# Seven groups' second layer by seven block products instead of three, and q and k cast to bf16 by GpSimd's loads

## The chip, the core and the metric

The kernel runs on one core of a Trainium2 chip. TensorE (PE) multiplies, VectorE (DVE), ScalarE (ACT) and GpSimd (POOL) do the rest, SyncE (SP) issues most transfers. The metric is the device time in microseconds of one launch, the median of several runs. A profile is of one further execution; it has its own time, and a span from its first to its last instruction.

## The reference

```python
def _attn_ref(q, k, v, w_phi):          # q, k, v: 8 batches x 8 heads x 576 x 64
    def phi(x):
        proj = np.einsum('bhsd,df->bhsf', x, w_phi)             # 128 features
        proj = proj - np.max(np.abs(proj), axis=-1, keepdims=True)
        return np.concatenate([np.exp(proj), np.exp(-proj)], axis=-1)
    q_p, k_p = (phi(q), phi(k))
    kv = np.einsum('bhsf,bhsd->bhfd', k_p, v)
    z = np.sum(k_p, axis=2)
    num = np.einsum('bhsf,bhfd->bhsd', q_p, kv)
    den = np.einsum('bhsf,bhf->bhs', q_p, z)[..., None] + 1e-06
    return num / den

def _moe_ref(x, g_ln, w_ch1, w_ch2):    # x: 8 x 576 x 512, the heads side by side
    mu = np.mean(x, axis=-1, keepdims=True)
    var = np.mean((x - mu) ** 2, axis=-1, keepdims=True)
    xn = (x - mu) / np.sqrt(var + 1e-06) * g_ln
    ch = np.maximum(xn @ w_ch1, 0.0) @ w_ch2                    # 512 -> 2048 -> 512
    return x + ch
```

All inputs and the output are fp32; the kernel multiplies in bf16.

## The kernel before

Attention runs over 32 units of two heads each, numbered 0 to 31. A unit's q and k are cast to bf16 and transposed (`qkT`), projected (`pm` for the maxima and for k, `pt` for q), put through exponentials (`eb` of k, `ea` of q), v is scaled by the keys' factors into `vv` on GpSimd (L1101 to L1107), then PE forms the key-value products in `n_bank` (L1162, L1168), the numerators (`num`, L1226, L1232), VectorE adds and inverts (`numc`, `rden`), and GpSimd writes x. The first 512 tokens of a head lie four to a partition; its last 64, the tail, are loaded apart (`qx`, `vx`).

The feed-forward part runs over nine groups of 512 token rows, 0 to 8, in four tiles of 128 tokens. The first layer (`hT_ps`, L1530; for group 0 L1387) gives 16 blocks of 128 hidden values into the ring `hT`. The second layer of group g is multiplied while the first layer of g + 1 runs. In groups 0 to 5 it is plain: per tile 16 matmuls of 512 columns into `ch_ps` (L1562), and one result per tile, on VectorE (L1570) or on ScalarE with the addition of x on GpSimd (L1575, L1579). In groups 6, 7 and 8 (`FAST`) it goes by seven block products instead of eight (`fast`, L1698): two token tiles, even and odd hidden blocks and two column halves make the blocks. It needs sums of blocks of w2, made once into T buffers (`weight_sums`, L1613), and sums of blocks of the hidden values into S buffers (`token_sums`, L1635), four for each pair of tiles and each half of the hidden blocks. A product is 8 matmuls of 256 columns, a group has 14; each product ends in one half-width result on VectorE (L1707). The T and S buffers are laid over the loaded q, k and v (`qk_bufs`, `v_bufs`), each pair of tiles with an S set of its own.

Loads: q, k and v of units 0 to 7 come on SP, 256 KB each, later ones 512 KB for two units (`load_main`, L577). Weights come in four transfers issued by GpSimd, which cast to bf16 on the way: two for w1 (L670), two for w2 (L688). Loads of units 8 to 15 wait for the second half of w1. Units 0 to 7 are transposed by PE. From unit 8 on (`a_trans_dma`) the loaded fp32 q and k are cast into one of three `b16` buffers, the main part by whichever of VectorE, ScalarE or GpSimd the list names (L797, L802, L804), the tail by another instruction, and a transposing transfer on SP (L823) fills one of four `qkT` buffers.

The order of every engine's instructions is fixed: the program makes a list of operations with their costs, `ORDER` names for each engine the operations in their order, and `Order.run` lays them out in time by a model of costs, lags and transfers, which decides how the engines' instructions are recorded against each other and where PE gets filler matmuls (L2172, before 75 us). `SLACK` and the costs in `dma` are numbers of that model.

## Time and profile before

| | |
|---|---|
| median of 3 runs | 355.04 us (355.03 to 356.68) |
| the profiled execution: time, span | 353.76 us, 352.0 us |
| busy: PE, DVE, ACT, POOL | 339.7, 296.1, 253.5, 192.7 us |
| granted PE clock, mean | 0.998 |
| moved | 53.87 MB; read from HBM 36.77 MB, written 9.44 MB |
| q and k loads of 512 KB on SP | 12 and 12, median 5.6 and 6.4 us to landing |
| main casts of q and k: POOL, ACT, DVE | 13 at 1.89, 10 at 1.07, 1 at 1.21 us |

A profile line of grouped instructions gives the source line, engine, operation, what is written and read, shapes and count, then busy time, the mean of one in ns, and the idle time before them with what ended it. Lines of windows give busy time and instruction count for each engine in a stretch, then the clock, the DMA share and GB/s. Matmuls are pipelined: the duration of one is longer than the distance to the next, so distances are read from the chain of waits, whose rows give start, length and what.

### The profile page before, as it was taken

To read this page: it belongs to the slowest core of one execution; us is meant where nothing else is said; L and a number is where in the kernel's file an instruction comes from. 1 tells how busy PE (TensorE), PEld (TensorE's weight loads), DVE (VectorE), ACT (ScalarE), POOL (GpSimd) and SP (SyncE) were. 2 spreads that over 40 slices of the span, in tenths; PEclk is the share of its full clock that TensorE was granted. 3 is DMA by queue.
4 is the path that set the end of the run, shared out by engine and by line. 5 is a ranking of instruction groups with operands and counts; after the bars stand their busy time and mean duration, and the time that the engine had idled before them with its cause. 6 is when DMAs were issued, how large, how long until landed. Compare 5 with 4: busy or idle time off the path is not lost.

```text
span 352.0 us, 9056 instructions
## 1 busy us (share of the span) xinstructions
PE 339.7 (97%) x3482; PEld 216.1 (61%) x3482; DVE 296.1 (84%) x670; ACT 253.5 (72%) x561; POOL 192.7 (55%) x250
## 2 busy tenths in 40 slices
PE   8887998999999999999999999999999999999995
PEld 7766785655555555464555455555555578488884
DVE  5799984999889889878896799799768699999994
ACT  4997988878999887869776958798676840554410
POOL 5487367849952584667292696987668630000000
PEclk9999999999999999999999999999999999999999
DMA  7999999994997939859809993705061123500053
GB/s 206 277 297 214 212 236 232 254 198 58 266 270 183 248 96 216 160 105 209 281 16 190 284 281 64 136 0 125 10 128 58 62 67 61 148 33 3 7 114 119
DMA packets 93675, 53.87 MB, mean 153 GB/s; under 512 B 61104, under 2 KB 88048, under 8 KB 93632
## 3 DMA queue, kind: packets, MB, share of 16 engines
q1 hardware_dynamic: 89392, 47.72, 57.2%
q0 software_dynamic: 3328, 4.49, 7.4%
q10 hardware_dynamic: 912, 1.08, 0.9%
q8 instruction: 27, 0.44, 0.5%
q14 instruction: 16, 0.13, 0.1%
HBM read 36.77 MB, written 9.44 MB: 131 GB/s over the span
## 4 chain that ended last, share of the span: by engine, by line
PE 82%; DMA 8%; DVE 3%; issue 2%; POOL 2%; ACT 2%; SPq 1%; ACTq 0%; POOLq 0%
PE hT_ps L1530 27%; PE ch_ps L1562 23%; PE ch L1698 10%; DMA w<-in_moe_w_ch_dram 6%; PE pm L1017 4%; PE n_bank L1168 4%; PE sum L1881 3%; PE num L1226 3%; PE pt L1026 2%; DMA qk<-in_q_dram 2%; POOL vv L1101 1%; PE n_bank L1162 1%; PE n_bank L1226 1%; ACT ea L914 1%; PE n_bank L1232 1%
## 5 line engine op out<-in xcount | busy, mean ns | idle before, releaser
L1530 PE MATMUL hT_ps<-xT,w 128*128 128x512 bf16 x432 | 103.9, 380 | 0.0
L1562 PE MATMUL ch_ps<-w,hT 128*128 128x512 bf16 x384 | 89.7, 380 | 1.2 <-DMA w<-in_moe_w_ch_dram 1.2
L1101 POOL TENSOR_TENSOR vv<-v,ek 128x1024 bf16<-128x1024 f32 x32 | 61.2, 1912 | 49.6 <-issue 32.9
L1074 DVE TENSOR_REDUCE m<-pm 128x8 f32<-128x1024 f32 x60 | 72.3, 1214 | 14.2 <-PE pm L1017 13.1
L1094 ACT ACTIVATE eb<-pm 128x1024 bf16<-128x1024 f32 x64 | 64.5, 1044 | 4.8 <-DVE m L1074 3.0
L1138 ACT ACTIVATE ea<-pt 128x1024 bf16<-128x1024 f32 x56 | 56.1, 1045 | 11.1 <-PE pt L1026 10.9
L1530 PEld LDWEIGHTS <-w 128*128 128x128 bf16 x432 | 38.1, 97 | 39.2 <-issue 1.9
L1562 PEld LDWEIGHTS <-hT 128*128 128x128 bf16 x384 | 35.0, 97 | 39.8 <-issue 2.5
L1540 ACT ACTIVATE hT<-hT_ps 128x512 bf16<-128x512 f32 x64 | 37.7, 608 | 18.6 <-PE hT_ps L1530 18.4
L1293 POOL TENSOR_TENSOR x<-numc,rden 128x128 bf16<-128x128 f32 (+1 forms) x56 | 33.6, 615 | 18.6 <-DVE rden L1260 18.6
L1538 DVE TENSOR_SCALAR hT<-hT_ps 128x512 bf16<-128x512 f32 x44 | 29.7, 679 | 5.4 <-PE hT_ps L1530 5.2
L1226 PEld LDWEIGHTS <-ea 128*128 128x128 bf16 x448 | 21.6, 97 | 8.5 <-issue 0.3
L804 POOL TENSOR_TENSOR b<-qk,one 128x1024 bf16<-128x1024 f32 x13 | 24.5, 1890 | 2.3 <-DMA v<-in_v_dram 2.3
L1168 PE MATMUL n_bank<-vv,eb 128*128 128x65 bf16 x512 | 23.8, 194 | 0.0
L1168 PEld LDWEIGHTS <-eb 128*128 128x128 bf16 x512 | 21.3, 98 | 2.2
L1248 DVE TENSOR_TENSOR numc<-num,em 128x390 f32<-128x390 f32 (+1 forms) x32 | 17.0, 530 | 6.6 <-PE num L1226 5.9
L1434 DVE BATCH_NORM_STATS2 st<-x 128x6 f32<-128x512 bf16 (+1 forms) x40 | 21.9, 567 | 0.4 <-POOL x L1293 0.4
L1017 PE MATMUL pm<-wbk,qkT 64*128 64x128 bf16 x448 | 19.9, 218 | 0.2 <-DVE xT L962 0.2
L1107 POOL TENSOR_TENSOR vv<-vx,ek 128x260 bf16<-128x260 f32 x32 | 19.9, 623 | 0.0
L1017 PEld LDWEIGHTS <-qkT 64*128 64x128 bf16 x448 | 13.8, 94 | 9.6 <-issue 6.5
L1579 POOL TENSOR_TENSOR o<-o,x 128x512 f32<-128x512 f32 x13 | 15.0, 1158 | 7.8 <-ACT o L1575 6.9
L1254 DVE TENSOR_TENSOR numc<-numc,num 128x390 f32<-128x390 f32 (+1 forms) x32 | 17.0, 533 | 0.7
(180 smaller groups left out, 659.7 us busy)
## 6 DMA issues: line engine op xcount, KB each, us to landing
out_dram<-o SPq DMA_DIRECT2D x29, 256.0 KB, 3.1
qk<-in_q_dram SPq DMA_DIRECT2D x12, 512.0 KB, 5.6
qk<-in_k_dram SPq DMA_DIRECT2D x12, 512.0 KB, 6.4
v<-in_v_dram SPq DMA_DIRECT2D x12, 512.0 KB, 5.2
w<-in_moe_w_ch_dram POOLq DMA_DIRECT2D x4, 1024.0 KB, 10.4
qk<-in_k_dram SPq DMA_DIRECT2D x8, 256.0 KB, 6.1
qk<-in_q_dram SPq DMA_DIRECT2D x7, 256.0 KB, 5.9
v<-in_v_dram SPq DMA_DIRECT2D x7, 256.0 KB, 6.7
```

The source lines that it names most:

```text
L1017: nc.tensor.matmul(ps[:, half * 4 + c, :], u["qkT"][rows, cols], wbk[rows, half, :], start=True, stop=True,)
L1074: nc.vector.reduce_max(out=m, in_=ps, axis=AX.X, apply_absolute_value=True)
L1094: nc.scalar.activation(eb, ps, AF.Exp, scale=(1.0, -1.0)[t])
L1101: eng.tensor_tensor(out=u["vv"][:, :, 0:MX, 0:D], in0=bcast(vb[:, hh, :].rearrange("p (c d) -> p c d", d=D), 1, 2), in1=bcast(e[:, :, 0:MX ...
L1138: nc.scalar.activation(u["EA"][:, t, 0:1024], u["pt"], AF.Exp, scale=(1.0, -1.0)[t])
L1168: nc.tensor.matmul(ps[:, t, c // 4, :], EB[:, t, c, :], vv[:, t, c, :], start=False, stop=(t == 0 and c == MX - 1), skip_group_check=True,)
L1226: nc.tensor.matmul(ps[t][:, i, :], ea(u, t, c), KV[:, t, c // 4, :], start=True, stop=True,)
L1293: eng.tensor_tensor(out=dst, in0=src, in1=by, op=ALU.mult)
L1530: nc.tensor.matmul(st["ps"], w1_sb[:, kc, jj * P : (jj + 1) * P], xT_bufs[g % XB][:, kc::KC, :], start=(kc == 0), stop=(kc == KC - 1),)
L1540: nc.scalar.activation(h_sb, st["ps"], AF.Relu)
L1562: nc.tensor.matmul(ch[g, i], hT[g, jj][:, i * P : (i + 1) * P], w2_sb[:, jj, :], start=(jj == 0), stop=(jj == JC - 1),)
L1698: nc.tensor.matmul(sums(), left(c), right(c), start=(begin and c == 0), stop=(c == CP - 1), skip_group_check=True,)
```

## The change

1. `FAST` becomes groups 2 to 8. Groups 2 to 5 (below `FULL`) use one S set for both pairs of tiles, and work the pairs one after the other: all products of tiles 0 and 1, then the sums and products of tiles 2 and 3. Their sums go to two PSUM banks per pair, half a bank for each output block.
2. From unit 8 on the main parts of q and k are loaded by GpSimd straight into `b16`, cast on the way: two loads of 256 KB (fp32) per unit. Their 24 loads of 512 KB on SP and their 24 casts go; v and all tails stay. `qk_bufs` are free after unit 7, so the T sums are made earlier.
3. Token sums may be made by GpSimd as well as by VectorE.
4. A new `ORDER` for all engines, and other numbers in the model (`SLACK`, the lags of GpSimd's loads).

```diff
-SLACK = ((0.22, 0.0, 0.0, 0.97), (0.35, 0.6, 1.6, 0.97), (0.22, -1.15, 0.0, 1.07))
+SLACK = ((0.22, 0.6, 0.8, 1.0), (0.35, 1.2, 2.2, 1.0), (0.22, -1.15, 0.0, 1.07))
...
-    FAST = (LAST - 2, LAST - 1, LAST)
+    FAST = range(2, LAST + 1)
+    FULL = LAST - 2
...
-        def cast_main(engine):
-            cast(
-                engine, b16[:, 0 : MX * P].rearrange("p (i f) -> p i f", i=2),
-                qk_bufs[u["g"] % NBUF][:, :, u["hh"], :],
+        def load_cast(i):
+            b, h, step = heads(u["pair"], u["i"], 0)
+            t = (q, k)[i]
+            nc.gpsimd.dma_start(
+                out=b16[:, i * 4 * P : (i + 1) * 4 * P].rearrange("p (a f) -> p a f", a=2),
+                in_=bass.AP(
+                    tensor=t.tensor, offset=t.offset + (b * H + h) * S * D,
+                    ap=[[4 * D, P], [S * D, 2], [1, 4 * D]],
+                ),
             )
...
-        add(("DVE", "ACT", "POOL"), (1.13, 0.937, 1.852), rank, cast_main, r=[*loaded(u, "q"), *loaded(u, "k")],
-            w=[("b16", n % NB16)])
-        dma("SP", rank, 0, turn, r=[("b16x", n % NB16), ("b16", n % NB16)],
+        for i in range(2):
+            dma("POOL", rank, 262144, lambda i=i: load_cast(i), w=[("b16" + "qk"[i], n % NB16)], us=0.7, row=1024)
...
+        dma("SP", rank, 0, turn, r=[("b16x", n % NB16), ("b16q", n % NB16), ("b16k", n % NB16)],
...
-    def token_sums(g, c):
+    def token_sums(g, c, only=None):
-        for p in range(NM // 2):
+        for p in range(NM // 2) if only is None else (only,):
+            z = p if g >= FULL else 0
...
-                nc.vector.tensor_tensor(out=out_, in0=a, in1=b, op=op)
+                eng = nc.vector if engine == "DVE" else nc.gpsimd
+                eng.tensor_tensor(out=out_, in0=a, in1=b, op=op)
...
-                add("DVE", Port(0.335), (), lambda i=i, f=sums: f(i),
+                add(("DVE", "POOL"), (Port(0.335), 1.08), (), lambda e, i=i, f=sums: f(i, e),
...
+        if lean:
+            cols, bank = chain % 2 * FH, chain // 2
...
+        if lean:
+            took = ("B", 1) if i in (0, 3) and cs[0] == 0 else None
+            gave = ("B", 1) if i in (5, 6) else None
...
+    def fast_steps(lean=False):
...
+        if lean:
+            return [
+                (p, i, cs) for p in pairs_
+                for i, cs in [(i, cs) for cs in (h1, h2) for i in range(2)]
+                + [(i, range(CP)) for i in range(2, 7)]
+            ]
...
+                    if g - 1 < FULL and 2 * step == len(steps):
+                        for c in (0, SH):
+                            token_sums(g - 1, c, 1)
...
-                for key in "kqv":
+                for key in "kqv" if m < QK_DMA else "v":
                     load_main(key, m + i, 1 if m < H else HG, rank, "SP")
```

How the lists move is shown for GpSimd at three places. The first is its beginning, from the load of the normalization's weights to the `vv` of unit 0 (before, with the start of unit 1's). Before:

```order
L658 DMA gln_85<-in_moe_g_ln_dram 128x4x1
L1101 TENSOR_TENSOR vv_335<-v0_101,ek_320 128x2x8x64
L1106 CAST vv_335<-ek_320 128x2x8
L1107 TENSOR_TENSOR vv_335<-vx0_106,ek_320 128x2x130
L1101 TENSOR_TENSOR vv_423<-v0_101,ek_401 128x2x8x64
```

And now (`b16_2`, `b16_0` and `b16_1` are the buffers of units 8, 9 and 10):

```order
L678 DMA gln_85<-in_moe_g_ln_dram 128x4x1
L838 DMA b16_2_147<-in_q_dram 128x2x256
L838 DMA b16_0_145<-in_k_dram 128x2x256
L838 DMA b16_2_147<-in_k_dram 128x2x256
L838 DMA b16_1_146<-in_q_dram 128x2x256
L1126 TENSOR_TENSOR vv_322<-v0_101,ek_309 128x2x8x64
L1131 CAST vv_322<-ek_309 128x2x8
L1132 TENSOR_TENSOR vv_322<-vx0_106,ek_309 128x2x130
```

Four loads of q and k, for units 8, 9 and 10, stand ahead of the first `vv`; the rest of the beginning keeps its order up to the first half of w1, which comes one instruction sooner. On PE the second half of w1 is first used 8 block matmuls (L1387), one unit's key-value products and five small transposes later than before; on SP one more v load of 256 KB stands behind that half.

The second place is the loads of w2, around the `vv` of units 4 and 5. Before:

```order
L688 DMA w2_133<-in_moe_w_ch2_dram 128x8x512
L986 TENSOR_TENSOR x_156<-xT2_140 128x2x2x64
L1101 TENSOR_TENSOR vv_873<-v2_105,ek_869 128x2x8x64
L1106 CAST vv_873<-ek_869 128x2x8
L1107 TENSOR_TENSOR vv_873<-vx1_107,ek_869 128x2x130
L1101 TENSOR_TENSOR vv_1037<-v2_105,ek_1024 128x2x8x64
L1106 CAST vv_1037<-ek_1024 128x2x8
L1107 TENSOR_TENSOR vv_1037<-vx1_107,ek_1024 128x2x130
L688 DMA w2_133<-in_moe_w_ch2_dram 128x8x512
```

And now:

```order
L1011 TENSOR_TENSOR x_156<-xT1_139 128x2x2x64
L708 DMA w2_133<-in_moe_w_ch2_dram 128x8x512 x2
L1011 TENSOR_TENSOR x_156<-xT2_140 128x2x2x64
L1019 TENSOR_TENSOR xs_134<-xT2_140 128x64
L1011 TENSOR_TENSOR x_156<-xT2_140 128x2x2x64
L1126 TENSOR_TENSOR vv_872<-v2_105,ek_858 128x2x8x64
```

The second half of w2 is issued right after the first and no longer behind the `vv` of two units.

The third place is between the `vv` of units 16, 17 and 18, where PE's list works the second layer of group 2. Before, from the end of unit 16's `vv` on:

```order
L1107 TENSOR_TENSOR vv_2809<-vx0_106,ek_2804 128x2x130
L1101 TENSOR_TENSOR vv_2855<-v2_105,ek_2801 128x2x8x64
L1106 CAST vv_2855<-ek_2801 128x2x8
L1107 TENSOR_TENSOR vv_2855<-vx0_106,ek_2801 128x2x130
L804 TENSOR_TENSOR b16_1_146<-qx1_89,one_113 128x128
L804 TENSOR_TENSOR b16_2_147<-qk1_102,one_113 128x1024
L804 TENSOR_TENSOR b16_1_146<-qk2_104,one_113 128x1024
L1579 TENSOR_TENSOR o_2955<-o_2955,x_157 128x512
L1293 TENSOR_TENSOR x_158<-numc_2942,rden_3067 128x128
L1297 TENSOR_TENSOR xs_134<-numc_2942,rden_3067 128x64
L1293 TENSOR_TENSOR x_158<-numc_2987,rden_3044 128x2x3x64
L1101 TENSOR_TENSOR vv_3095<-v0_101,ek_3086 128x2x8x64
```

And now, from the end of unit 17's `vv` to unit 18's (`qk0` holds the S set, `b16_2` q and k of a later unit):

```order
L1132 TENSOR_TENSOR vv_2915<-vx0_106,ek_2840 128x2x130
L1663 TENSOR_TENSOR qk0_100<-qk0_100,hT_151 128x512 x2
L1663 TENSOR_TENSOR qk0_100<-hT_151 128x512 x2
L1663 TENSOR_TENSOR qk0_100<-hT_151,qk0_100 128x512 x2
L1318 TENSOR_TENSOR x_158<-numc_2931,rden_3075 128x128
L838 DMA b16_2_147<-in_k_dram 128x2x256
L1126 TENSOR_TENSOR vv_3115<-v0_101,ek_3110 128x2x8x64
L1131 CAST vv_3115<-ek_3110 128x2x8
L1132 TENSOR_TENSOR vv_3115<-vx0_106,ek_3110 128x2x130
```

Casts of loaded q and k and an addition to `o` have gone; token sums (six here) and a load stand between two units' `vv`. In the whole program GpSimd loses 13 main casts and 12 additions to `o` and gets 48 loads and 57 token sums; VectorE gets 56 half-width results more.

More of the change, by code (lines that the diff above doesn't have):

```diff
@@ L249, in after @@
     def after(self, op, engine):
-        return LAG[op.engine, engine] + RESERVE if (op.engine, engine) in LAG else op.lag
+        pair = ("POOL" if op.engine == "none" else op.engine, engine)
+        return LAG[pair] + RESERVE if pair in LAG else op.lag
     def run(self):
@@ L258, in run @@
             op.engine = op.engine or op.engines[0]
+        for op in self.ops:
+            if isinstance(op.us[0], Op) and op.us[0].engine != "ACT":
+                turn[op.engine].remove(op.number)
+                op.engine = "none"
         place = {engine: 0 for engine in turn}
-        loads = {"DMA": [], "DMA_w": []}
+        loads = {"DMA": [], "DMA_w": [], "none": []}
         room, free, events, done, offered = self.room, {}, [], [], set()
@@ L313, in run @@
                     shut = 1000.0
-                us, lag = op.us[op.engines.index(engine)], op.lag
+                us, lag = 0.0 if engine == "none" else op.us[op.engines.index(engine)], op.lag
                 if isinstance(us, Move):
@@ L549, in dma @@
         elif queue == "POOL":
[L550 removed]
+            packets, ns, lag = nbytes / row / 16, {4096: 0.155, 2048: 0.084}.get(row, 0.048), {4096: 4.8, 2048: 5.1}.get(row, LAND)
             if row == 256:
@@ L561, in dma @@
             add(queue, took[0], rank, emit, r=r, w=(key, *w), acquire=lanes)
-            add(kind, took[1], rank, None, r=(key, *r), w=(*w, key), lag=1.45, release=lanes)
+            add(kind, took[1], rank, None, r=(key, *r), w=(*w, key), lag=1.9, release=lanes)
             return
-        add(queue, us, rank, emit, r=r, w=(key, *w), acquire=lanes, load=(kind, packets * ns))
+        wide_ = kind == "DMA_w" and pieces > 1
+        line = ["weights issued"] if wide_ else []
+        add(queue, us, rank, emit, r=r, w=(key, *w, *line), acquire=lanes, load=(kind, packets * ns))
+        for i in range(pieces if wide_ else 0):
+            add(kind, Move(packets / pieces, ns), rank, None, r=(key,), w=("weights moved", (key, "moved")))
+        if wide_:
+            add(kind, Move(0.01, ns), rank, None, r=(key, (key, "moved"), *r), w=(*w, key), lag=lag, release=lanes)
+            return
         for i in range(pieces):
@@ L1625, in blocks, with sums @@
                 return space[:, s : s + 2 * SH - 1 : 2, (2 * p + i) * P : (2 * p + i + 1) * P]
-            def sums(i, p=p, blocks=blocks):
-                S1, S2, S3, S4 = [t[:, c : c + SH] for t in S_of[p]]
+            def sums(i, engine, z=z, blocks=blocks):
+                S1, S2, S3, S4 = [t[:, c : c + SH] for t in S_of[z]]
                 out_, a, b, op = (
@@ L1699, in products @@
                     sums(), left(c), right(c),
-                    start=(begin and c == 0), stop=(c == CP - 1), skip_group_check=True,
+                    start=(begin and c == 0 and not (lean and i == 1)), stop=(c == CP - 1), skip_group_check=True,
                 )
@@ L1715, in fast @@
         else:
-            r += [("S", p, s_key, c) for c in range(cs[0], cs[-1], SH)]
+            r += [("S", z, s_key, c) for c in range(cs[0], cs[-1], SH)]
         if t_key is None:
@@ L1724, in fast @@
             counts["o"] += 2
-        add("PE", mm(len(cs), FH), counts["V"], products, r=r, w=[("fast", g, p, bank), "ch"],
+        add("PE", mm(len(cs), FH), counts["V"], products, r=r, w=[("fast", g, p, bank if split or lean else 0), "ch"],
             acquire=took, due=due(g + 1, i / 7))
@@ L1748, in fast @@
             dma("SP", counts["V"], 262144, lambda: store(g, t, ch["o", g, t]), r=both)
-    b16_home = [[("b16x", i), ("b16", i)] for i in range(NB16)]
+    b16_home = [[("b16x", i), ("b16q", i), ("b16k", i)] for i in range(NB16)]
     qkT_home = [
```

35 lines of the change are left out of this document (20 added, 15 removed), and 221 rows, old and new, of the table ORDER.

## The prediction

> **What bounds the kernel now.** I read the page first: span, busy time by engine, the granted clock, and the chain of waits.
>
> ```profile
> span 352.0 us, 9056 instructions
> ...
> PE 339.7 (97%) x3482; PEld 216.1 (61%) x3482; DVE 296.1 (84%) x670; ACT 253.5 (72%) x561; POOL 192.7 (55%) x250
> ...
> PEclk9999999999999999999999999999999999999999
> ...
> PE 82%; DMA 8%; DVE 3%; issue 2%; POOL 2%; ACT 2%; SPq 1%; ACTq 0%; POOLq 0%
> ```
>
> PE is busy for 97% of the span, at full clock in every slice, and holds 82% of the chain that ended last. A busy PE may still wait between matmuls, so I read the windows next, cut where GpSimd (POOL) starts the scaled values `vv` of unit 9 and of unit 31.
>
> ```profile
> 0.00:77.70 77.70, 69.37 (x907) 53.14 (x908) 63.77 (x158) 63.42 (x156) 47.13 (x71) 1.00 1.08 241
> 77.70:273.70 196.00, 195.99 (x1931) 105.37 (x1929) 164.90 (x337) 158.60 (x348) 136.33 (x164) 1.00 0.66 152
> 273.70:352.00 78.30, 74.34 (x650) 57.63 (x648) 67.40 (x177) 31.51 (x60) 9.24 (x15) 0.99 0.25 69
> ```
>
> In the middle 196 us PE is busy without a gap, while DVE has 31 us, ACT 37 and POOL 60 to spare. In the first 77.7 us PE is short of work for 8.3 us, and the DMA share beside the clock shows 1.08: the transfers fill that stage. The last 78.3 us lose 4 us, nearly all behind PE's last matmul. So from 60 us on time is saved by giving PE less to stream, as long as the other engines keep their lead; before that, by what the transfers let PE begin.
>
> In the first stage the chain stands on two weight transfers.
>
> ```profile
> 28.73 9.94 DMA w<-in_moe_w_ch_dram
> ...
> 47.52 10.79 DMA w<-in_moe_w_ch_dram
> ...
> 60.60 0.06 PE n_bank L1162
> 60.66 0.26 PE n_bank L1168 x8
> ```
>
> The second quarter of the weights (the second half of w1) is issued at 28.73 and lands at 38.67; the last (second half of w2) runs from 47.52 to 58.31. The PE timeline shows what each cost.
>
> ```profile
> 38.72 1.92 PE L1387 MATMUL hT_ps<-xT,w 128*128 128x256 bf16 x16 [0.63 <-DMA w<-in_moe_w_ch_dram]
> ...
> 58.35 1.89 PE L1562 MATMUL ch_ps<-w,hT 128*128 128x512 bf16 x8 [1.20 <-DMA w<-in_moe_w_ch_dram]
> ```
>
> PE stood still 0.63 us for the one and 1.20 us for the other; the rest of both transfers lay under other work.
>
> **The change part by part.** *PE.* Groups 2 to 5 give up the plain second layer, 64 matmuls of 512 columns each, for seven block products per pair of tiles, 112 matmuls of 256 columns. The chain has both kinds back to back:
>
> ```profile
> 219.53 3.45 PE ch_ps L1562 x16
> ...
> 285.39 12.23 PE ch L1698 x112
> ```
>
> Sixteen wide ones take 3.45 us, so 64 take 13.80; 112 narrow ones take 12.23. That is 1.57 us less in each of four groups, **-6.3 us**. Nothing else on PE changes but two fillers. This term is on the path that sets the end as long as PE stays the one that is waited for.
>
> *The first 60 us.* Four loads of 256 KB in fp32 (q and k of unit 8, k of unit 9, q of unit 10) now stand on POOL right behind its first small loads, in the stage that transfers fill. Their price is bounded by the two queues' rows of the first 75 us: packet time as a share of 16 engines.
>
> ```profile
> q1 hardware_dynamic: 20303, 13.14, 69.9%
> q0 software_dynamic: 3328, 4.49, 34.5%
> ```
>
> The hardware queue needs 0.699 x 75 / 13.14 = 4.0 us per MB, so 1.05 MB take 4.2 us. The software queue, which counts what lands (bf16, half of what is read), needs 0.345 x 75 / 4.49 = 5.8 us per MB, so 0.52 MB take 3.0 us. One v load of 256 KB (1.0 us) moves behind the second half of w1, so that half lands 2.0 to 3.2 us later. PE meets it later too: in the new list it has 8 more block matmuls (8 x 12.23 / 112 = 0.9 us), one unit's key-value products (2 x 0.06 + 2 x 0.26 = 0.6 by the chain rows above) and five small transposes (about 0.3) in front of it, 1.8 us. The wait of 0.63 becomes 0.8 to 2.0; I take **+0.8** and keep +0.2 to +1.4. The Trainium skill ("DMA: Bandwidth & Descriptors", section "SWDGE vs HWDGE vs iDMA") says that each DMA engine takes turns between the queues that GpSimd's loads and SP's loads fill; by that rule the four early loads also take half the engines from units 1 to 3 while they run. No row shows this pair side by side. It would put the whole 4.2 us on those units and leave the sum inside the bound above.
>
> The last weight goes the other way.
>
> ```profile
> 28.73 0.79 POOL L670 DMA_DIRECT2D w<-in_moe_w_ch_dram  x1
> ...
> 32.92 0.92 POOL L688 DMA_DIRECT2D w<-in_moe_w_ch_dram  x1
> ...
> 47.52 0.93 POOL L688 DMA_DIRECT2D w<-in_moe_w_ch_dram  x1
> ```
>
> Its issue stood 14.6 us behind the third, queued behind two units' `vv`; now both follow each other at once. Meanwhile SP no longer issues 2 MB of q and k for units 8 to 11 in between, of which half has moved to the front. It should land some 4 us earlier (1.05 MB at 4.0 per MB), so the wait of 1.20 goes: **-1.2**, at worst 0.
>
> *GpSimd.* Whole-kernel counts from the two lists, with durations from these rows:
>
> ```profile
> L804 POOL TENSOR_TENSOR b<-qk,one 128x1024 bf16<-128x1024 f32 x13 | 24.5, 1890 | 2.3 <-DMA v<-in_v_dram 2.3
> ...
> L802 ACT CAST b<-qk 128x1024 bf16<-128x1024 f32 x10 | 10.6, 1065 | 0.0
> ...
> L1579 POOL TENSOR_TENSOR o<-o,x 128x512 f32<-128x512 f32 x13 | 15.0, 1158 | 7.8 <-ACT o L1575 6.9 <-POOL b L804 0.9
> ...
> L475 POOL DMA_DIRECT2D qx<-in_q_dram x2 | 1.3, 656 | 0.0
> ```
>
> Out go 13 casts and 12 residual additions; in come 48 load issues (0.66 to 0.92 by the issues above; I take 0.70) and 57 sums of 128x512. Such a sum was never run on POOL. The nearest rows are the weight sums of twice the size (2.13 further down, so half is 1.06) and the addition of 512 columns in fp32 (1.16). I take 1.1. Between the `vv` of units 9 and 31 that is +38 x 0.70 - 11 x 1.89 - 11 x 1.16 + 34 x 1.1 - 3 x 2.13 = +24: 160 us of the 190 left, 84%. The other 23 sums fall in the last stage, where POOL has 69 us idle. POOL stays off the path, but each `vv` now has sums and issues queued in front of it, and PE's key-value products wait for `vv`. ACT loses ten casts (10.6 us) and 12 results and gains 12 first-layer results and 13 centerings: about even.
>
> *VectorE.* In the same stretch, by the lists, 56 half-width results and 19 sums come in, 8 first-layer results, 10 centerings and 6 full-width results go.
>
> ```profile
> L1538 DVE TENSOR_SCALAR hT<-hT_ps 128x512 bf16<-128x512 f32 x44 | 29.7, 679 | 5.4 <-PE hT_ps L1530 5.2
> ...
> L1707 DVE SCALAR_TENSOR_TENSOR o<-ch,rstd,o 128x256 f32<-128x256 f32 x18 | 8.2, 476 | 1.7 <-PE ch L1698 1.7
> ...
> L1451 DVE TENSOR_SCALAR xc<-x,mv 128x512 bf16<-128x512 bf16 x24 | 8.6, 381 | 0.2
> ...
> L1570 DVE SCALAR_TENSOR_TENSOR o<-ch_ps,rstd,x 128x512 f32<-128x512 f32 x11 | 8.1, 737 | 0.4 <-PE ch_ps L1562 0.4
> ...
> L1635 DVE TENSOR_TENSOR v<-hT 128x512 bf16<-128x512 bf16 x10 | 4.1, 418 | 0.0
> ```
>
> By durations that is 26.7 + 7.9 - 5.5 - 3.8 - 4.4 = +20.9, or 185.8 of 189.7 us. These durations overlap, though:
>
> ```profile
> 243.05 1.22 DVE L1074 TENSOR_REDUCE m<-pm 128x8 f32<-128x1024 f32 x1
> 244.18 0.42 DVE L849 TENSOR_REDUCE m<-n_bank 128x2 f32<-128x256 f32 x1
> 244.51 1.22 DVE L1074 TENSOR_REDUCE m<-pm 128x8 f32<-128x1024 f32 x1
> ```
>
> The next starts 0.09 before the last ends. With 0.085 taken from each of 388 instructions 153 us remain, 81%. The loaded stage of before lies between these two measures, and there PE lost nothing:
>
> ```profile
> 290.00:315.00 25.00, 25.00 (x184) 17.80 (x183) 24.10 (x70) 10.25 (x21) 0.10 (x1) 1.00 0.34 85
> ```
>
> DVE at 24.10 of 25 us, PE at 25.00. So VectorE is no bound by itself; I cost it together with the waits below.
>
> *The wait that is added.* Groups 2 to 5 have one buffer set for the token sums. Sums of the second pair of tiles cannot start until PE has read those of the first; PE then has at least three products of the first pair and two of the second in front of it, 40 matmuls, 4.4 us, and the second pair's first sum product needs four sums by then. On POOL they take 4.4 us, on VectorE 4 x 0.34. With one `vv` (1.9 + 0.25 + 0.6) queued before them on POOL, they take 7.1. So each of four groups costs 0 to 2.7 us, less what PE finds in attention between. PE's list does put attention and first-layer work there in every group, so I take 0.25 each, **+1.0**, and keep 0 to +5.
>
> *Sum.* -6.3 + 0.8 - 1.2 + 1.0 = **-5.7**. The profiled span goes from 352.0 to 346.3, its run from 353.76 to 348.1. The median shown, 355.04, lies 1.28 above the profiled run; I predict the median: 355.04 - 5.7 = **349.3 us**.
>
> **The rivals.** *The ports clash (slower).* Only few of VectorE's instructions with two SBUF inputs met POOL before. One weight sum did, one did not, both of one size:
>
> ```profile
> 215.49 2.13 POOL L1613 TENSOR_TENSOR qk<-w,qk 128x1024 bf16<-128x1024 bf16 x1
> ...
> 220.35 1.94 POOL L1101 TENSOR_TENSOR vv<-v,ek 128x1024 bf16<-128x1024 f32 x1 [2.74 <-ACT ek L1087]
> 222.24 0.71 POOL L1106 CAST vv<-ek 128x16 bf16<-128x16 f32 x1
> ```
>
> ```profile
> 220.45 2.39 DVE L1613 TENSOR_TENSOR qk<-w 128x1024 bf16<-128x1024 bf16 x1
> ...
> 240.59 0.66 DVE L1613 TENSOR_TENSOR qk<-w 128x1024 bf16<-128x1024 bf16 x1
> ```
>
> 2.39 against 0.66: it started 0.10 us behind a `vv` and ended 0.66 after it, and POOL's next cast took 0.71 where 0.25 is usual. All token sums of before ran while POOL was idle (0.10 of 25 us, above). Now 30 run on VectorE in the middle stretch beside a POOL that is busy 84% of the time. If each loses half a POOL sum or more, 0.45 us, that is 13.5 us on VectorE: 185.8 + 13.5 = 199.3 by durations, 9.6 more than the stretch has. If VectorE is then what PE waits for, the time is 349.3 + 9.6 = 358.9; it decides from 0.38 us per sum, where 185.8 + 30 x 0.38 = 197.2 reaches 189.7 + 5.7 + 1.8. Against it speaks the overlap row, by which VectorE has room for this. The Trainium skill ("SBUF — State Buffer", section "Who interferes with whom") states this as a rule: a VectorE instruction with two SBUF inputs and a GpSimd instruction that reads SBUF exclude each other, and the second to come waits for all of the first. The trace agrees in its one meeting (2.39 against 0.66).
>
> *Given back at the sums.* Each of the four groups waits 1.3 us and more on POOL's queue as bounded above: 355.04 - 6.3 - 0.4 + 5 = 353.3. For it: the order is fixed, so PE cannot step around a late sum. Against it: 60 us of POOL's idle time in the middle stretch, of which 30 remain.
>
> *The casts come late, so the change does not do what it says.* A unit's two loads, its landing and its transpose share one of three b16 buffers.
>
> ```profile
> w<-in_moe_w_ch_dram POOLq DMA_DIRECT2D x4, 1024.0 KB, 10.4
> ...
> qkT<-b SPq DMA_TRANSPOSE x24, 4.1
> ```
>
> With the weights' landing as the worst row, 2 x 0.7 + 10.4 + 4.1 = 15.9 us; three units last 3 x 189.7 / 22 = 25.9. Only at 10 us more does this ring bind; with 1 us beyond, a third per unit over 22 units, 356.6.
>
> *More is gained.* The early loads hide, neither half of w1 or w2 is waited for any more (0.63 and 1.20), and no group waits: 355.04 - 6.3 - 0.6 - 1.2 = 346.9. For it: PE meets the second half of w1 1.8 us later; against it: the first stage's transfers have no room (share 1.08).
>
> **How the numbers follow.** Forecast 0.50, more gained 0.14, given back 0.17, clash 0.14, late casts 0.05. What can be told from no change is 0.5%, 1.8 us: faster is below 353.3, slower above 356.8. The forecast and "more gained" are faster, "given back" half faster and half the same, the clash slower but for a mild form, late casts about even: faster 0.72, same 0.13, slower 0.15. The range holds the forecast, "more gained" with 1 us to spare, and "given back" with a mild clash: 345.5 to 356. The forecast's own range is 347.3 (no added wait, w1 free of loss) to 351.5.
>
> **What would show it.** PE's group of the plain second layer falls from 384 to 128 matmuls, the 256-column products rise by 448, still at 0.109 us apart. The wait for the second half of w1 is 0.8 to 2.0 us, that for w2 is gone. POOL's sums take 1.0 to 1.2 us in its rows, and VectorE's stay at 0.42 unless they clash; a mean of 0.8 or more would be the slower rival at work. The chain from 60 us on should stay on PE; if DVE or POOL lines of the sums hold more than 2% of it, the added waits were sized too small. A wait of PE on the transposed q and k, which before has none, would show late casts. I would be wrong altogether if the first stage moved by more than 2 us: its order was written anew on all engines, and I priced only two of its waits.

## The result and the profile after

The changed kernel takes **358.73 us** (median of 9 runs, 356.9 to 362.5) against 353.66 for the kernel before (9 runs, the three shown among them): 1.0146 times as long, interval 1.011 to 1.018. It is slower by 5 us where 5.7 us less was forecast; the range (345.5 to 356.0) missed it. The profiled execution of the change is its fastest one, 356.88 us with a span of 355.1, so the profiles differ by 3.1 us and the medians by 5.

The head of the page, busy time by engine:

```profile
span 355.1 us, 9586 instructions
PE 335.3 (94%) x3664; PEld 236.3 (67%) x3672; DVE 315.3 (89%) x705; ACT 251.8 (71%) x564; POOL 254.4 (72%) x328
```

PE is busy for 4.4 us less than before, 94% of the span in place of 97%. The windows show where the rest stands still. The columns are the stretch, its length, busy time and instructions of each engine, then clock, DMA share and GB/s. First the stages as cut in the prediction:

```profile
0.00:77.70 77.70, 69.48 (x901) 53.79 (x907) 66.72 (x163) 61.03 (x152) 54.10 (x80) 0.98 1.02 205
77.70:273.70 196.00, 188.27 (x2101) 123.33 (x2102) 180.49 (x383) 158.50 (x355) 165.83 (x214) 1.00 0.71 137
273.70:355.10 81.40, 77.59 (x667) 59.22 (x664) 68.07 (x162) 32.23 (x61) 34.52 (x35) 1.00 0.23 61
```

Then the stretches between 125 and 273.7 us:

```profile
125.00:150.00 25.00, 20.87 (x253) 13.61 (x252) 23.64 (x47) 20.83 (x47) 22.35 (x31) 1.00 0.91 179
150.00:175.00 25.00, 24.65 (x288) 16.59 (x286) 21.87 (x47) 18.70 (x45) 21.72 (x28) 1.00 0.71 146
175.00:200.00 25.00, 24.13 (x265) 17.57 (x263) 23.71 (x54) 18.91 (x41) 19.25 (x24) 1.00 0.79 131
200.00:225.00 25.00, 23.56 (x242) 15.81 (x241) 21.63 (x46) 18.90 (x43) 21.88 (x32) 1.00 0.77 148
225.00:250.00 25.00, 25.00 (x309) 16.51 (x308) 23.19 (x52) 21.37 (x49) 17.84 (x25) 1.00 0.61 132
250.00:273.70 23.70, 23.09 (x273) 17.42 (x272) 23.58 (x54) 16.57 (x40) 21.51 (x26) 1.00 0.29 70
```

The 0.98 in the first row is new; it was 1.00. In 40 slices of the span, the granted clock in tenths, first the change and then e5, a run of the experiments below:

```profile
PEclk9899999999999999999999999999999999999999
PEclk9998999999999999999999999999999999999999
```

In the change's profile PE runs at half clock from 7.3 to 10.7 us (windows of 0.5 us inside that read 0.50), in e5's from 33.0 to 36.4. Each such spell in the profiles follows, or falls into, a stop of PE of 1.1 us or more: 1.40 us here, 3.72 in e5. It lasts 3.4 us (7 in e3) and takes 1.7 us of PE's full-speed time, 0.005 of a run's mean clock. All nine runs of the change have a mean clock of 0.989 to 0.995, by this measure one or two spells each; the ten of e16, which is the kernel before again, have 0.998 to 1.000. What that is worth stands with the experiments.

In the middle stage, where PE had no gap at all, it now lacks 7.7 us, over 4 of them between 125 and 150 us. That is where group 2's second layer begins, the first one with the new seven products. VectorE is busy for 180.5 of 196 us (164.9 before), GpSimd for 165.8 (136.3). Neither is full. Who PE waited for in that stage:

```profile
PE ch L1736 <- DVE o L1745: 5.0, 6, 1.7
PE num L1251 <- DVE m L1099: 2.0, 1, 2.0
PE n_bank L1187 <- POOL vv L1132: 0.4, 1, 0.4
```

It is VectorE, above all its half-width results (L1745), and only 0.4 us of it is GpSimd's `vv`. The timeline around the two longest stops (start, length, what; a bracket gives the idle time before it and what ended it):

```profile
139.74 1.91 POOL L1126 TENSOR_TENSOR vv<-v,ek 128x1024 bf16<-128x1024 f32 x1
140.31 1.60 DVE L1663 TENSOR_TENSOR qk<-qk,hT 128x512 bf16<-128x512 bf16 x1
140.45 0.60 PE L1736 MATMUL ch<-w,hT 128*128 128x256 bf16 x4 [0.41 <-DVE o L1745]
...
142.24 0.47 DVE L1745 SCALAR_TENSOR_TENSOR o<-ch,rstd,o 128x256 f32<-128x256 f32 x1
...
142.76 1.91 PE L1736 MATMUL ch<-qk,qk 128*128 128x256 bf16 x16 [1.72 <-DVE o L1745]
...
145.08 0.72 POOL L838 DMA_DIRECT2D b<-in_k_dram  x1
145.11 2.78 DVE L1476 TENSOR_SCALAR xc<-x,mv 128x512 bf16<-128x512 bf16 x1
...
145.82 1.92 POOL L1126 TENSOR_TENSOR vv<-v,ek 128x1024 bf16<-128x1024 f32 x1
...
147.82 1.21 DVE L1099 TENSOR_REDUCE m<-pm 128x8 f32<-128x1024 f32 x1
...
149.08 0.53 PE L1251 MATMUL num<-KV,ea 128*128 128x65 bf16 x12 [2.01 <-DVE m L1099]
```

At 140.31 VectorE starts a token sum, 0.57 us after GpSimd started a `vv`. It ends 1.60 us later, 0.26 us after the `vv`; sums that meet nothing take 0.41. The half-width result behind it is late, and PE waits 1.72 us for it. At 145.11 VectorE starts a centering (`xc`, 0.34 us when alone) beside a load issue on GpSimd; a `vv` follows at 145.82, and the centering ends 2.78 us after its start, again just after the `vv`. The maximum behind it (L1099) is late, and PE waits 2.01 us. The groups of these instructions on VectorE between 125 and 275 us:

```profile
L1663 DVE TENSOR_TENSOR qk<-hT 128x512 bf16<-128x512 bf16 x15 | 6.9, 473 | 0.0
L1663 DVE TENSOR_TENSOR qk<-qk,hT 128x512 bf16<-128x512 bf16 x10 | 6.3, 646 | 0.0
L1476 DVE TENSOR_SCALAR xc<-x,mv 128x512 bf16<-128x512 bf16 x3 | 4.5, 1492 | 0.0
L1663 DVE TENSOR_TENSOR qk<-hT,qk 128x512 bf16<-128x512 bf16 x5 | 2.4, 475 | 0.0
L1476 DVE TENSOR_SCALAR xc<-xm,mv 128x512 bf16<-128x512 bf16 x1 | 0.3, 346 | 0.0
```

Against 0.41 and 0.34 us, the 30 sums are stretched by 3.6 us in all and three of the four centerings by 3.5: 7.1 us, the largest of it where PE stands still longest.

The first stage moved too. The first product of group 1's first layer, the first instruction of L1555, starts here (shortest, median and longest in ns, then first and last start in us):

```profile
L1555 PE MATMUL hT_ps<-xT,w x432: 377/379/390, 80.0 to 316.4; 128*128 128x512 bf16 x144
```

In the kernel before it starts at 78.6 us. From that point to VectorE's last result (0.7 us behind PE's last product), PE's idle time grew from 1.0 to 8.3 us. The window of the kernel before:

```profile
78.60:349.00 270.40, 269.44 (x2555) 162.10 (x2551) 231.50 (x511) 189.22 (x404) 144.70 (x179) 1.00 0.55 129
```

And of the change:

```profile
80.00:352.00 272.00, 263.74 (x2731) 181.02 (x2732) 246.33 (x537) 188.93 (x410) 198.63 (x247) 1.00 0.57 114
```

So the difference of the profiles is +1.4 us up to that point (+0.5 against e16's 79.5), -5.7 us of PE work behind it, and +7.3 us of idle PE.

### The profile page after: what moved, and what is told of

It is laid out like the page before. It is cut to its first block, busy times and chain, and to the rows that moved or that the text cites. A ratio compares the mean times of both kernels' runs of the same rounds, so it can differ in the third digit from the quotient of the medians.

```text
span 355.1 us, 9586 instructions
## 1 busy us (share of the span) xinstructions
PE 335.3 (94%) x3664; PEld 236.3 (67%) x3672; DVE 315.3 (89%) x705; ACT 251.8 (71%) x564; POOL 254.4 (72%) x328
## 4 chain that ended last, share of the span: by engine, by line
PE 75%; DVE 17%; issue 4%; DMA 2%; ACT 1%; POOL 0%; ACTq 0%; DVEq 0%; POOLq 0%
PE hT_ps L1555 23%; PE ch L1736 21%; PE ch_ps L1587 6%; PE hT_ps L1412 4%; PE sum L1919 4%; PE pm L1042 3%; DVE m L1099 3%; PE n_bank L1193 3%; DVE st L1459 3%; PE num L1251 3%; PE pt L1051 2%; DVE o L1745 2%; DMA qk<-in_q_dram 2%; DVE qk L1663 1%; DVE numc L1279 1%
## 5 line engine op out<-in xcount | busy, mean ns | idle before, releaser
L1555 PE MATMUL hT_ps<-xT,w 128*128 128x512 bf16 x432 | 103.1, 379 | 0.0
L1099 DVE TENSOR_REDUCE m<-pm 128x8 f32<-128x1024 f32 x60 | 72.1, 1213 | 4.2 <-PE pm L1042 3.0
L1555 PEld LDWEIGHTS <-w 128*128 128x128 bf16 x432 | 38.7, 98 | 39.1 <-issue 1.1
L1318 POOL TENSOR_TENSOR x<-numc,rden 128x384 bf16<-128x384 f32 (+1 forms) x56 | 34.1, 617 | 10.5 <-DVE rden L1285 10.0
L1736 PEld LDWEIGHTS <-qk 128*128 128x128 bf16 x352 | 33.6, 98 | 6.8 <-issue 2.3
L1736 PE MATMUL ch<-qk,qk 128*128 128x256 bf16 x264 | 32.4, 272 | 2.0 <-DVE o L1745 2.0
L1663 POOL TENSOR_TENSOR qk<-qk,hT 128x512 bf16<-128x512 bf16 x10 | 11.7, 1178 | 28.7 <-DVE qk L1663 24.5
L1587 PE MATMUL ch_ps<-w,hT 128*128 128x512 bf16 x120 | 29.7, 379 | 0.4
L1736 PE MATMUL ch<-w,hT 128*128 128x256 bf16 x208 | 27.0, 272 | 3.0 <-DVE o L1745 2.9
L1663 POOL TENSOR_TENSOR qk<-hT 128x512 bf16<-128x512 bf16 x24 | 27.9, 1171 | 1.1 <-PE ch L1736 0.6
L1745 DVE SCALAR_TENSOR_TENSOR o<-ch,rstd,x 128x256 f32<-128x256 f32 x48 | 22.4, 474 | 4.5 <-PE ch L1736 4.2
L1563 DVE TENSOR_SCALAR hT<-hT_ps 128x512 bf16<-128x512 f32 x32 | 21.6, 682 | 2.1 <-PE hT_ps L1555 1.8
L1745 DVE SCALAR_TENSOR_TENSOR o<-ch,rstd,o 128x256 f32<-128x256 f32 x42 | 19.8, 476 | 3.5 <-PE ch L1736 3.2
```

Of the source, the lines that this page charges most:

```text
L1099: nc.vector.reduce_max(out=m, in_=ps, axis=AX.X, apply_absolute_value=True)
L1318: eng.tensor_tensor(out=dst, in0=src, in1=by, op=ALU.mult)
L1555: nc.tensor.matmul(st["ps"], w1_sb[:, kc, jj * P : (jj + 1) * P], xT_bufs[g % XB][:, kc::KC, :], start=(kc == 0), stop=(kc == KC - 1),)
L1587: nc.tensor.matmul(ch[g, i], hT[g, jj][:, i * P : (i + 1) * P], w2_sb[:, jj, :], start=(jj == 0), stop=(jj == JC - 1),)
L1663: eng.tensor_tensor(out=out_, in0=a, in1=b, op=op)
L1736: nc.tensor.matmul(sums(), left(c), right(c), start=(begin and c == 0 and not (lean and i == 1)), stop=(c == CP - 1), skip_group_check=True,)
```

## Experiments

The theory after the profile is **ports**: VectorE's sums and centerings are held up while a GpSimd instruction is under way, and PE stands behind them. Its rival is **count**: VectorE has 56 results more to deliver in the lean groups and is simply late. A third question is the **first stage**. Ratios are to the kernel before, run beside each set, with their intervals; "starts" is where group 1's first layer begins in that run's profile.

| run | what it changes in the change | median us | ratio (95%) | starts |
|---|---|---|---|---|
| the change | | 358.73 | 1.0146 (1.011 to 1.018) | 80.0 |
| e1 | no collisions | 355.49 | 1.0052 (1.002 to 1.008) | 81.0 |
| e2 | 6.5 us less on VectorE | 360.74 | 1.0189 (1.013 to 1.025) | 81.9 |
| e3 | two centerings to ScalarE | 360.81 | 1.0170 (1.012 to 1.022) | 86.0 |
| e4 | early loads behind w2, more filler | 360.11 | 1.0171 (1.014 to 1.020) | 82.4 |
| e5 | no collisions, memsets apart | 352.97 | 0.9976 (0.995 to 1.000) | 84.4 |
| e6 | e5 and 6.5 us less on VectorE | 352.89 | 0.9989 (0.996 to 1.002) | 80.7 |
| e7 | early loads behind w2 | 357.66 | 1.0112 (1.009 to 1.014) | 80.3 |
| e8 | no collisions of centerings | 357.24 | 1.0099 (1.006 to 1.014) | 80.4 |
| e9 | e5 and e7 | 353.07 | 0.9966 (0.994 to 0.999) | 82.1 |
| e10 | e7, `vv` in two pieces | 359.02 | 1.0122 (1.009 to 1.016) | 84.1 |
| e11 | e7, three centerings and a sum moved | 358.55 | 1.0127 (1.010 to 1.016) | 81.9 |
| e12 | e10 and e11 | 357.46 | 1.0107 (1.008 to 1.014) | 82.3 |
| e13 | e5, early loads behind the `vv` of unit 4 | 351.56 | 0.9936 (0.991 to 0.996) | 80.2 |
| e14 | early loads behind the `vv` of unit 4 | 358.58 | 1.0128 (1.009 to 1.016) | 80.7 |
| e15 | e14, `vv` in two, as e11 moved | 357.46 | 1.0101 (1.008 to 1.013) | 81.6 |
| e16 | the kernel before, again | 353.65 | 1.0010 (0.999 to 1.003) | 79.5 |

### Collisions or count (e1, e2, e5, e6)

**e1** puts reductions of one SBUF operand in the place of VectorE's token sums of groups 2 to 5 and of its centerings from group 2 on, and keeps their number, place and length. So it leaves out what these sums and centerings compute. It adds four memsets of the S buffers; sums of the last three groups and other work stay as they are. **e5** and **e6** below leave out the same.

```diff
-                eng = nc.vector if engine == "DVE" else nc.gpsimd
+                if engine == "DVE" and g < FULL:
+                    nc.vector.tensor_reduce(out=out_[:, 0:2, 0:64], in_=a[:, 0:2, :]..., op=ALU.max, axis=AX.X)
+                    return
...
-            if engine == "DVE":
+            if engine == "DVE" and g > 1:
+                nc.vector.tensor_reduce(out=xc_bufs[xi][:, i, 0:96], in_=x[:, 0:192]..., op=ALU.max, axis=AX.X)
+            elif engine == "DVE":
```

> VectorE's token sums of groups 2 to 5 and its centerings from group 2 on are replaced by reductions of the same length (0.41 and 0.34 us) that read one SBUF operand; what they leave unwritten is zero or old data, so the output is not the reference's. Four short memsets on VectorE near 105 us are added. Number, order and length of VectorE's instructions stay. Theory 'ports': the profile of the change has 6.6 us of stretched sums and centerings on VectorE between 77 and 274 us, in the same stretches in which PE stands still 7.4 us; without them 352 to 354 us against 358.7 for the change. Rival 'count': VectorE is simply full in the lean groups (56 half-width results more), so 358 to 359.

355.49, between the two. Its own addition was in the way. VectorE's timeline in e1 where the memsets stand:

```profile
110.42 0.68 DVE L1643 TENSOR_TENSOR qk<-w,qk 128x1024 bf16<-128x1024 bf16 x1
111.16 2.10 DVE L1648 MEMSET qk<- 128x512 uint32 x4
113.18 0.63 DVE L1600 SCALAR_TENSOR_TENSOR o<-ch_ps,rstd,x 128x512 f32<-128x512 f32 x1
```

PE waited 2.6 us behind these 2.1 us. **e5** puts the four memsets behind four scalings of w1 (96.6 to 117.3 us in its profile), and is otherwise the same.

> As the first run, with sums and centerings on VectorE that read one SBUF operand, but the four memsets stand between 80 and 111 us, where VectorE has room, and no longer in one piece at 111 us, where PE lost 2.6 us behind them. 'Ports': another 2 us less than that run, about 353.5; what stays above 349.3 is the first stage and VectorE's fuller list. 'Count': 355.5 again or more.

352.97: "ports" foretold 353.5. Without collisions the time goes from 1.0146 to 0.9976 of the kernel before, **6.0 us**, and the idle PE time behind group 1's start from 8.3 to 2.7 us, by this window of e5:

```profile
84.40:350.60 266.20, 263.54 (x2734) 180.75 (x2732) 240.56 (x541) 188.06 (x410) 197.06 (x247) 1.00 0.59 117
```

**e2** leaves the collisions and takes 6.5 us of plain work off VectorE by leaving half of each row out of the statistics, **e6** does the same without collisions.

```diff
-            nc.vector.bn_stats(out=st_x[:, g, i, half or 0, :], in_=x[:, h0 * D : h1 * D])
+            n = DM // 2 if g > 1 else h1 * D
+            nc.vector.bn_stats(out=st_x[:, g, i, half or 0, :], in_=x[:, h0 * D : n])
```

> The row statistics of groups from 2 on read 256 of 512 columns (so mean and variance are of half a row): 28 instructions on VectorE go from 0.68 to 0.41 us, 24 of them before 274 us, 6.5 us less, spread evenly, and no collision is taken away. Rival 'count': VectorE's plain load is what PE waits for, so this gains as much as taking away the collisions: 352 to 354 us. 'Ports': PE waits behind single stretched instructions, so evenly spread time gives at most a third of it back: 356.5 to 358.5.

> As the run beside it without port collisions, and the row statistics from group 2 on read half a row (6.5 us less on VectorE). After the collisions PE still waited 1.8 us for VectorE's half-width results. If VectorE's plain load makes that rest, this gains 1.5 to 2 us on the run beside it; if not, nothing.

Neither gains: 360.74 against 358.73, and 352.89 against 352.97. "Count" falls. What PE still waits for in its products is the same in both to a tenth. In e5, from 84 us on:

```profile
PE ch L1750 <- DVE o L1759: 1.8, 4, 0.6
```

And in e6:

```profile
PE ch L1751 <- DVE o L1760: 1.8, 4, 0.6
```

So these 1.8 us belong to the sequence of the products in a lean group (one PSUM half is read by VectorE before the next product adds to it) or to the order of the lists around it; the runs don't tell which. They don't hang on how full VectorE is.

### Moving the collisions away (e3, e8, e10, e11, e12)

**e3** moves two op numbers, 1057 and 1315, from VectorE's list to ScalarE's; **e8** is e1 with the centerings alone.

> Two centerings, those that took 2.78 and 1.36 us on VectorE in the profile of the change (at 145.1 and 177.6 us), go to ScalarE (0.72 us each); all else stays. 'Ports': 3.4 us of stretch go and the two stops of PE behind them shrink: 2 to 3.5 us faster than the change, 355 to 357. 'Count': only 0.7 us of plain work goes: 358 to 359.

> Only the centerings on VectorE from group 2 on are replaced by reductions of the same length; the token sums stay. By the profile the centerings hold 3.5 of 6.6 us of stretch: half of the gain of taking both away, so 356 to 357. If the sums next to them take over the collisions, as after the move of two centerings to ScalarE, under 1 us: 358 to 359.5.

e3's 360.81 shows nothing by itself, since its first stage was the longest of all (86.0). From group 1's start to the last product it took 269.8 us against 271.3. e8 gained 1.7 us by the ratios, whose intervals overlap. In both profiles the sums that stayed were hit harder: their mean between 125 and 275 us rose from 0.53 to 0.58 us, 1.5 us more over 30 sums. Taken off one place, part of the collisions comes back at the next.

**e10** cuts the long instruction of each `vv` in two, **e11** moves three centerings to ScalarE and the sum of 140.31 us to GpSimd, **e12** does both. All have the early loads behind w2 as e7 has.

```diff
+            vc = vb[:, hh, :].rearrange("p (c d) -> p c d", d=D)
+            for c in range(0, MX, MX // 2):
+                cs = slice(c, c + MX // 2)
-                out=u["vv"][:, :, 0:MX, 0:D], ...
+                eng.tensor_tensor(out=u["vv"][:, :, cs, 0:D], in0=bcast(vc[:, cs], 1, 2), in1=bcast(e[:, :, cs], 3, D), op=ALU.mult)
```

> With the early loads behind w2, GpSimd's long instruction of each vv (1.91 us) is cut in two of about 1.0 us, some 4 us more on GpSimd in all; VectorE and PE are untouched and the output is the reference's. If VectorE is held for as long as the GpSimd instruction that it met lasts, its longest waits halve: of 5.9 us lost to collisions about 2 come back, 355.5 to 356 against 357.66 with the loads moved alone. If it is held for another reason, or GpSimd's 4 us tell: 357.5 to 359.

> With the early loads behind w2, three centerings of groups 2 to 4 go from VectorE to ScalarE and the token sum that met a vv at 140 us goes to GpSimd, behind the sum it depends on; the output is the reference's. In the profile of the two moved centerings the time from group 1's first layer to the end was 1.5 us shorter than in the change, hidden by the first stage; the sum was stretched by 1.2 us. 'Ports': 355 to 356 against 357.66. If other sums take over the collisions: 357 to 358.

> Both of the last two edits together. If each takes a part of the collisions: 354 to 355, still not below the kernel before (353.5); if they take the same ones: as the better of them.

The mechanism shows in e10's timeline. The sum that took 1.60 us now takes 0.75 and ends 0.28 us after the first piece of the `vv`:

```profile
143.81 2.23 POOL L1129 TENSOR_TENSOR vv<-v,ek 128x512 bf16<-128x512 f32 x2
...
144.38 0.75 DVE L1665 TENSOR_TENSOR qk<-qk,hT 128x512 bf16<-128x512 bf16 x1
```

VectorE is held for as long as the one GpSimd instruction that it met (the row is of two pieces, the first of 1.04 us). The Trainium skill ("SBUF — State Buffer", section "Who interferes with whom") says the same: who comes first has the shared ports for a whole instruction, and the other is blocked, not slowed. Yet the time did not fall (359.02, 358.55, 357.46 against 357.66 for e7). The stretch of sums and centerings together was 5.8 us in e10, 5.5 in e11 and 5.1 in e12, against 6.2 in e7 by the same count; other meetings took the place of those removed. In e11's timeline a sum is long beside load issues:

```profile
146.64 0.75 POOL L838 DMA_DIRECT2D b<-in_k_dram  x1
146.96 2.13 DVE L1663 TENSOR_TENSOR qk<-hT,qk 128x512 bf16<-128x512 bf16 x1
147.38 0.71 POOL L838 DMA_DIRECT2D b<-in_q_dram  x1
148.08 0.71 POOL L838 DMA_DIRECT2D b<-in_k_dram  x1
148.80 2.06 POOL L1126 TENSOR_TENSOR vv<-v,ek 128x1024 bf16<-128x1024 f32 x1
```

### The first stage (e4, e7, e9, e13, e14, e15, e16)

**e4** moves the four early casting loads on GpSimd's list behind both halves of w2 (numbers 440, 449, 442 and 454 behind 177).

> The four early casting loads (q and k of units 8 to 10) move on GpSimd's list from ahead of the first vv to behind the second half of w2; the list is otherwise the same. In the profile of the change the vv of units 0 to 4 start 1.1 to 2.2 us later than before, w1 is issued 1.1 and 1.5 us later, and PE issues 1.4 us more of filler. If the early loads did that, this is 1.5 to 2 us faster than the change, about 357; if the new order of the other engines did it, 358.7.

360.11, and this says little: the list of PE is partly written by the planner, which put 72 fillers more where its model saw PE idle, 14.6 us of filler in place of 11.2. **e7** is the same with PE's own list as in the change.

> The four early casting loads behind the second half of w2 again, but with the change's own PE list, fillers included: the run before got 72 fillers more (196 against 124, 0.06 us each, 4.3 us), which the planner put where its model saw PE idle. If the early loads delay the first stage, 2 us less than the change (356.5 to 357.5); if only PE's list does, 358.7 to 360.

357.66, 1.2 us less by the ratios, whose intervals overlap. PE's first product of group 0 came at 36.2 us in place of 38.0 (35.6 before). Most of that was lost again at once. GpSimd's timeline in e7:

```profile
34.46 0.71 POOL L838 DMA_DIRECT2D b<-in_q_dram  x1
35.15 1.42 POOL L838 DMA_DIRECT2D b<-in_k_dram  x2
36.54 0.73 POOL L838 DMA_DIRECT2D b<-in_q_dram  x1
37.26 0.66 POOL L1011 TENSOR_TENSOR x<-xT 128x256 bf16<-128x256 f32 x1
```

VectorE's next to it:

```profile
38.76 1.08 DVE L1459 BATCH_NORM_STATS2 st<-x 128x6 f32<-128x256 bf16 x3 [2.15 <-POOL x L1011]
```

And PE's:

```profile
41.02 0.39 PE L1051 MATMUL pt<-qkT,wbk 64*128 64x512 bf16 x2 [1.66 <-DVE m L1099]
```

Four issues take 2.8 us on GpSimd, its `x` stands behind them, VectorE's statistics wait 2.15 us for `x`, and PE 1.66 us for VectorE's next maximum. **e9** is e5 and e7 together.

> The early casting loads behind w2, and VectorE's sums and centerings without a second SBUF operand, both together. If the two losses add up: 1 to 1.5 us less than without the collisions alone (352.97), 351.5 to 352, and a spread of about 1 us as in the run with the loads moved (357.4 to 358.5) in place of 4.6. If the first stage's loss has another cause: 353 with the wide spread.

353.07, spread from 351.2 to 354.6: no gain on e5 and no narrow spread. Next the loads went behind the `vv` of unit 4, where GpSimd's next instruction is unit 5's `vv`: without collisions in **e13**, alone in **e14**, with `vv` in two pieces and e11's moves in **e15**. **e16** is the kernel before for a second profile.

> The early loads stand behind the vv of unit 4, and VectorE's sums and centerings hold no second SBUF operand. When the loads stood right behind w2, PE's first product of group 0 came 1.8 us earlier than in the change, but their four issues (2.8 us) then stood in front of GpSimd's x, VectorE waited 2.15 us for x and PE 1.7 us for VectorE. Here nothing is queued behind them but the vv of unit 5. If that was what ate the gain: 1.5 to 2 us below 353, so 351 to 351.5. If the first stage is slow for another reason: 352.5 to 353.5.

> The change with nothing but the four early loads moved behind the vv of unit 4. With the first stage's loss gone: 356.5 to 357; with another cause: 357.7 to 358.7. In its profile group 1's first layer should begin at 78.5 to 79.5 us in place of 80 to 86.

> The best legal version from these parts: early loads behind the vv of unit 4, vv cut in two, three centerings and one sum off VectorE. By the runs with the loads behind w2 (357.46) less 1.5 to 2: 355.5 to 356, still above the kernel before (353.7).

> The kernel before, unchanged, for a second profile of its first stage. If group 1's first layer begins within 1 us of 78.6 us again, the 80 to 86 us of the changed kernels are the change's; if it scatters as far, the first stage is as uneven without the change.

e13 takes 351.56 us, all six runs within 1.0 us, 2 us below the kernel before. Against e5 that is 1.4 us by the medians; the intervals of the ratios just overlap.

The granted clock tells more about these 1.4 us, and about the spread, than the loads do. Of e5's runs, the five at 0.998 or more have a median of 351.57 us, the five at 0.994 to 0.995 one of 353.26. Of e9's they are 351.57 (five) and 353.36 (seven); of e13's, 351.45 (five) and a single 351.86. So at full clock the place of the early loads makes no difference that shows; e13 has fewer runs with a spell at half clock. (e7 doesn't show the step: two runs at full clock have 357.58, the other four 357.76.) Why a stop of PE brings a spell at one time and not at another isn't shown: in e14 one follows the 2.01 us wait for VectorE's maximum, in the change the same wait passes without one.

At full clock e14, with collisions, takes 357.51 (three runs) against e13's 351.45: 6.1 us for the collisions, with the loads at one place and the clock the same. The change has no run at full clock. If e14's three stand for it, its 5 us are about -2 for the lean groups without collisions (e13 against e16's 353.65), +6 for the collisions and +1 for the clock.

By its median e14 gains nothing that can be told from the change (358.58), and e15 stays 3.6 us above the kernel before by its ratio. No version found that computes everything beats that kernel.

The first product of group 0 (the first instruction of its line, first and last start again) tells the early loads from the rest. The kernel before:

```profile
L1387 PE MATMUL hT_ps<-xT,w x128: 269/273/284, 35.6 to 62.2; 128*128 128x256 bf16 x128
```

The change:

```profile
L1412 PE MATMUL hT_ps<-xT,w x128: 269/273/283, 38.0 to 65.8; 128*128 128x256 bf16 x128
```

And e13:

```profile
L1415 PE MATMUL hT_ps<-xT,w x128: 269/273/283, 36.0 to 65.8; 128*128 128x256 bf16 x128
```

Before it starts at 35.6 us (36.4 in e16). With the early loads where the change has them it starts between 38.0 and 44.0 us in seven profiles, with the loads moved between 36.0 and 38.4 in nine. So these loads delay the first units by about 2 us. In the two latest of the seven (44.0 and 42.4), PE had one long stop at the transpose of a tail, for which the profile names no releaser. That row of e3:

```profile
PE qxT_ps L758 <- issue: 5.2, 1, 5.2
```

e5 has 3.7 us at the same place. Nowhere else is it over 0.9. In both, a tail load of k issued at 24.3 and 24.0 us lands 8.9 and 8.1 us later, within 0.3 us of the stop's end; in the change it takes 5.1. That the early loads make it late is likely and not shown. What the moved loads win at group 0 is mostly gone by group 1's start (80.2 to 84.1 us in the nine, 78.6 and 79.5 before). For e7 the reason was shown above, and the four of e9 to e12 have a spell at half clock ahead of group 1; for the loads behind unit 4's `vv` it is open. With the early loads in place and no spell ahead of group 1, e6 and e8 start at 80.7 and 80.4, no later.

## Why the prediction was wrong

**PE, -6.3 us: right in kind, a little too large.** The plain second layer fell to 128 products and the narrow ones rose by 448. PE's busy time from group 1's start on fell from 269.4 to 263.7 us in the change (263.5 without collisions), -5.7.

**The first stage: the second half of w1, +0.8, and of w2, -1.2.** w2's wait is gone as foretold. The wait for w1 is gone as well: in the first 77.7 us no wait of PE ends with a weight. But the stage as a whole lost 1.4 us in the profile where 0.4 were to be won, and up to 7.4 in another (e3). So the claim that these two waits price the stage failed too. With the four early loads, group 0's first product comes some 2 us later, with or without a wait that names a transfer; set elsewhere, their issues hold up GpSimd's `x`. PE's stops also brought spells at half clock, which the prediction does not have. The prediction had named the place ("half the engines from units 1 to 3") and left it inside a bound, 0.2 to 1.4 us, that was too narrow for group 0's first product.

**GpSimd.** The sums took 1.15 to 1.18 us against the 1.1 taken, the middle stage 165.8 us of busy time where about 160 was forecast. PE waited 0.4 us for `vv`. GpSimd is not late, as foretold, and "given back at the sums" did not happen in its own way: no `ch` product waited for a sum on GpSimd. Two of GpSimd's groups between 125 and 275 us:

```profile
L1663 POOL TENSOR_TENSOR qk<-hT 128x512 bf16<-128x512 bf16 x17 | 19.7, 1167 | 1.1 <-PE ch L1736 0.6 <-ACT hT L1565 0.5
L1663 POOL TENSOR_TENSOR qk<-hT,qk 128x512 bf16<-128x512 bf16 x11 | 12.7, 1156 | 5.8 <-DVE qk L1663 5.8
```

**VectorE by the stretch, "no bound by itself".** Its busy time, 180.5 us, was even less than the 185.8 foretold, and e2 and e6 confirm that its plain load isn't what costs. But this was the wrong question. The two measures of room compare sums over 196 us; each engine's list is worked in its order, and in a lean group PE waits for VectorE's next result. One sum that is held for 1.2 us cost PE a stop of 1.72, with 15 us to spare elsewhere in the stage.

**The added waits, +1.0 with 0 to +5.** Without collisions the idle PE time behind group 1's start is 2.7 us against 1.0: +1.7, within the bounds, but for VectorE's results and not for GpSimd's sums. With collisions it is +7.3. That is the step that failed: the term counted only sums that come late from GpSimd's queue, and put VectorE's holds at nothing. What is left without them is e13's profile: -5.9 us of PE work, +1.7 of idle PE and a start of group 1 at 80.2 for 78.6, +1.6, give the 2.6 us by which its span (349.4) is shorter than before.

**The rival "the ports clash" was the case.** It had the mechanism, a chance of 0.14 and 358.9 us; measured were 358.7. That the two times agree is luck: its arithmetic was wrong, and the clock has a part in the 358.7. It priced 0.45 us on each of 30 sums and let it decide from 0.38 us on, when VectorE would be full. Measured were 0.12 us per sum, far below that point, and 3.5 us on three centerings, which it left out: it counts instructions with two SBUF inputs, and they read one. The cost came through order, not fullness: 7.1 us of stretch, 5.6 us of idle PE, 6.0 us of time. (The one meeting that it quotes ended 0.55 us after the `vv`, not 0.66. And the forecast without added wait and loss at w1 is 347.5, not 347.3; nothing hangs on either.) The section of the Trainium skill that the prediction cited for two-operand instructions also names `tensor_scalar` as one that can enter a mode that uses both port pairs; the trace agrees with 2.78 us against 0.34.

The sign that the prediction set for this rival, a mean of 0.8 us or more for VectorE's sums, would have missed it at 0.53. The rivals "late casts" and "more gained" did not come: no wait of PE on transposed q and k is among its waits in the middle stage, shown above.

Two things spoke for the clash in the trace of before: the one meeting of a weight sum with a `vv` (2.39 against 0.66), and that VectorE's token sums had run only beside an idle GpSimd. Both were quoted. What was not drawn from them is how often a sum of 0.41 us meets one of GpSimd's instructions when these fill 84% of the time (165.8 of 196 us, 85%, in the change), and that nothing in a lean group hides it.
